# A fused attention and feed-forward backward pass: another opening on TensorE, and block-diagonal products without column tiles

## The chip, the core and the metric

The kernel runs on one core of a Trainium2 chip. The metric is the device time of one execution in microseconds (us); the median of the runs counts. The engines are TensorE (PE in the profile, its weight loads PEld), VectorE (DVE), ScalarE (ACT), GpSimd (POOL) and SyncE (SP, which issues most DMAs). TensorE writes its results to PSUM; a VectorE or ScalarE instruction copies them on to SBUF.

## The reference

The kernel computes a gated mix of a linear-attention block and a ReLU feed-forward block, together with all gradients. S is 2048, D is 640, there are 32 heads of 20, and the feed-forward width is 1728. All inputs are bf16.

```python
phi = lambda t: jnp.where(t > 0, t + 1, jnp.exp(t)) + 1e-6
q, k, v = split_heads(x @ wqkv)
pq, pk = phi(q), phi(k)
kv  = einsum("bhsd,bhse->bhde", pk, v);  z = einsum("bhsd->bhd", pk)
o   = einsum("bhqd,bhde->bhqe", pq, kv) / (einsum("bhqd,bhd->bhq", pq, z)[..., None] + 1e-6)
a   = merge_heads(o) @ wo
b   = relu(x @ w1) @ w2
g   = sigmoid((x * gate_w).sum(-1, keepdims=True))
out = g * a + (1 - g) * b
# outputs: out and its gradients for x, wqkv, wo, w1, w2, gate_w, given grad_out
```

## The kernel before

Rows of x are handled in 16 tiles of 128 (index `i`), columns of D in 5 chunks of 128 (index `k` or `m`). The work runs in stages, in this order: the key products of all 16 tiles (`k_part`) and two query tiles; the products of keys with x (`yp`); the forward blocks (`h_half`, `q_main`, `out_chunk`); the gradients of w2 (`w2p`); then the backward blocks, the gradients of w1, wq and wk, and that of x. Tiles in PSUM come from one pool, `PP`, with four buffers of two banks each: whoever wants a fifth waits until an earlier one has been copied out. Outside the opening the order of instructions on each engine is set by the framework's scheduler; each engine works through its own in order.

**The opening.** TensorE's order is written out by hand (L465 to L487, `manual_schedule`). It begins with products of a zeroed tile (`warm_up`, L445) that fill the time until data lands. `xt(i)` (L436) transposes the first five x tiles on TensorE: five transposes into a bf16 PSUM tile (`xtp`), then one copy to SBUF by `copy_out` (L347), on ScalarE for an even first argument and on VectorE otherwise. Between the warm-up and `xt(0)` stand one small transpose of the gate's weights (`gwtp`, L469) and a copy of five columns (L470) that makes the gate a 641st column of the key weights. `k_part(i, ks)` (L450) multiplies x tile `i` with the chunks `ks` of the key weights, 512 and 129 columns wide, accumulating in a PSUM tile `kp`. When a tile's last chunk is in, ScalarE takes two exponentials from it (L458 the gate, L395 in `phi_chain`), and VectorE finishes with L397 (bf16, SBUF to SBUF) and L398, which reads the PSUM tile a last time and so frees its buffer. The five chunks of the key weights are loaded one by one, 0 to 2 on ScalarE's queue and 3 and 4 on SyncE's. Tiles from 5 on are transposed by DMA (`xT_ld`); the first of these loads waits for `k_part(1, [2])`.

**GpSimd in the opening.** It builds the identity, then the masks of the heads: `MDw` (L493, L496 to L501) by 20 selects of 64x80, two for each 64-row half of a chunk, and `MDh` by 10 selects of 128x32 (L503, L505); nearly at the end it zeroes a matrix of 128x3200 (`KVT_s`, L507).

**Block-diagonal products.** Heads are 20 wide, so that a product of two 640x640 matrices is wanted only in blocks of 20 on the diagonal. `blockdiag` (L378) computes them by 64-row halves: for each chunk `m` and each `k`, two products with 64 stationary columns and 80 moving ones, which write partitions 0 to 63 and 64 to 127 of the same PSUM columns; VectorE multiplies the ten results with the mask (L390). It is called for `KVT_s` in the forward pass (L631) and for `dKVT_s` in `small_1` (L835).

**Window products.** `win_mms` (L366) multiplies with such a banded matrix: only the columns of each chunk's window (`WIN`: 0 to 140, 120 to 260, 240 to 400, 380 to 520, 500 to 640) are streamed. The 640 result columns are split at 320 over the two banks of a PSUM tile (`HD`), which cuts one window and gives six products of 140, 140, 80, 80, 140 and 140 columns. There are 20 such tiles: five in `mt_tile` (L634), five each in `small_0`, `small_2` and `small_3`. `halves` (L354) reads the two banks of 320 columns in one copy.

Of the kernel before, what the change touches and what calls it, by code (L numbers as in the profile page):

```python
# [8 lines left out]
ALU = mybir.AluOpType  # L9
AX = mybir.AxisListType  # L10
FP32 = mybir.dt.float32
BF16 = mybir.dt.bfloat16
PSUM = bass.MemoryType.PSUM

P = 128
H = 32
DH = 20
# [64 lines left out]
def kernel(  # L82
# [5 lines left out]
    nc = tc.nc  # L88
# [4 lines left out]
    S, D = x2.shape  # L93
    F = B_w1.shape[1]
    NT = S // P
    KD = D // P
# [6 lines left out]
    NG = NT // G  # L103
    assert NB * NBW == F and NB == 4 and D == H * DH and D % P == 0 and NT % 4 == 0 and FT < P
    WIN = _windows(D)
    BWID = max(-(-64 * (r + 1) // DH) * DH - 64 * r // DH * DH for r in range(2 * KD))
    DSPL = [(0, 512), (512, D)]
    DSP1 = [(0, 512), (512, D + 1)]
    DX = D + H
# [102 lines left out]
    xN = aview("xN", NT * DQX, i=NT)  # L212
    xN2 = aview("xN2", NT * D, i=NT)
    NPE = 5
# [7 lines left out]
    xTv = {i: (xT_view(i, i + 1), slice(0, P)) for i in range(NPE)}  # L222
# [8 lines left out]
    wk_s, wq_s, wv_s, wo_s = aview("wk", KD * DQX, k=KD), mat("wq"), mat("wv"), mat("wo")  # L231
# [5 lines left out]
    Y_s, YT_s, KVT_s, MT_s = mat("Y"), mat("YT"), mat("KVT"), mat("MT")  # L237
    M_s = aview("M", KD * D).rearrange("p (t c s) -> p t c s", t=KD, c=KD)
    dwoT_s, dwo_s = mat("dwoT"), mat("dwo")
    X_s, XT_s, woT_s, wvT_s, KV2_s = mat("X"), mat("XT"), mat("woT"), mat("wvT"), mat("KV2")  # L240
    dKV_s, dKVT_s, Q_s, N_s = mat("dKV"), mat("dKVT"), mat("Q"), mat("N")
# [19 lines left out]
    def gsl(i):  # L261
# [15 lines left out]
    cpool = ctx.enter_context(tc.tile_pool(name="const", bufs=1))  # L277
    tsb = ctx.enter_context(tc.tile_pool(name="ts", bufs=2))
    psp = ctx.enter_context(tc.tile_pool(name="ps", bufs=1, space=PSUM))
    ident = cpool.tile([P, P], BF16, name="ident")  # L280
    nc.gpsimd.memset(ident[:], 0.0)
    nc.gpsimd.affine_select(out=ident[:], in_=ident[:], compare_op=ALU.not_equal, fill=1.0, base=0,
                            pattern=[[-1, P]], channel_multiplier=1)
    gwb = cpool.tile([P, D], BF16, name="gwb")
    ones_sq = cpool.tile([P, P], BF16, name="ones_sq")
    zc_t = cpool.tile([P, KD], FP32, name="zc_t")
    MDw = cpool.tile([P, KD, BWID], BF16, name="MDw")
    MDh = cpool.tile([P, KD, H], BF16, name="MDh")
    zb = cpool.tile([P, D], BF16, name="zb")
    dzb = cpool.tile([P, D], BF16, name="dzb")  # L290
# [14 lines left out]
    def _nm(pfx):  # L305
        _cnt[0] += 1
        return f"{pfx}{_cnt[0]}"

    def pp(name="pp"):
        return psp.tile([P, 2, 512], FP32, tag="PP", bufs=4, name=_nm(name))  # L310
# [4 lines left out]
    def csl(i):  # L315
        return slice(i * P, (i + 1) * P)

    def flat(ps_tile):
        return ps_tile.rearrange("p b c -> p (b c)")
# [22 lines left out]
    def mm_cols(ps_tile, lhsT, rhs_fn, start, stop, spl=DSPL, **kw):  # L342
        for b, (a, e) in enumerate(spl):
            mm = nc.tensor.matmul(ps_tile[:, b, 0:e - a], lhsT=lhsT, rhs=rhs_fn(a, e), start=start, stop=stop, **kw)  # L344
        return mm

    def copy_out(n, dst, src):  # L347
        if n % 2 == 0:
            nc.scalar.copy(dst, src)  # L349
        else:  # L350
            nc.vector.tensor_copy(dst, src)

    HD = D // 2
    def halves(ap):  # L354
        return ap.rearrange("p (b c) -> p b c", b=2)

    SEGS = []
    for j, (lo, hi) in enumerate(WIN):
        if lo // HD == (hi - 1) // HD:
            SEGS.append((j, lo, hi))  # L360
        else:
            SEGS.append((j, lo, HD))
            SEGS.append((j, HD, hi))
    LASTSEG = {a // HD: n for n, (j, a, e) in enumerate(SEGS)}

    def win_mms(ps_tile, lhsT_fn, rhs_mat):  # L366

        seen = set()
        for n, (j, a, e) in enumerate(SEGS):
            bank = a // HD  # L370
            nc.tensor.matmul(ps_tile[:, bank, a - HD * bank:e - HD * bank], lhsT=lhsT_fn(j), rhs=rhs_mat[:, j, a:e],  # L371
                             start=bank not in seen, stop=LASTSEG[bank] == n, skip_group_check=True)
            seen.add(bank)

    HP = P // 2
    BW = [HP * r // DH * DH for r in range(2 * KD)]

    def blockdiag(dst, lhsT_mat, rhs_mat):  # L378

        ps = pp("bd")  # L380
        for m in range(KD):
            for k in range(KD):
                for h_ in range(2):
                    r = 2 * m + h_
                    nc.tensor.matmul(ps[h_ * HP:(h_ + 1) * HP, 0, m * BWID:(m + 1) * BWID],
                                     lhsT=lhsT_mat[:, k, r * HP:(r + 1) * HP], rhs=rhs_mat[:, k, BW[r]:BW[r] + BWID],
                                     start=(k == 0), stop=(k == KD - 1), skip_group_check=True)
        for r in range(2 * KD):
            m, hp = r // 2, slice(r % 2 * HP, r % 2 * HP + HP)
            nc.vector.tensor_tensor(dst[hp, m, BW[r]:BW[r] + BWID], ps[hp, 0, m * BWID:(m + 1) * BWID],  # L390
                                    MDw[hp, m, :], ALU.mult)

    def phi_chain(ps_flat, dst):
        eb = tmp("tb", 8)
# [39 lines left out]


    def xt(i):  # L436
        tp = psp.tile([P, KD, P], BF16, tag="PP", bufs=4, name=_nm("xtp"))
        for k in range(KD):
            nc.tensor.transpose(tp[:, k, :], xN[:, i, csl(k)], ident[:])
        copy_out(0 if i == 1 else 1, xTv[i][0], tp[:])  # L440

    def xT(i, k):
        return xTv[i][0][:, k, xTv[i][1]]

    def warm_up(n):  # L445
        for _ in range(n):
            nc.tensor.matmul(wp_[:, 0, :], lhsT=warm[:, 0:P], rhs=warm, start=True, stop=True)

    kps = {}

    def k_part(i, ks):
        if 0 in ks:
            kps[i] = pp("kp")
        kp = kps[i]
        for k in ks:
            mm = mm_cols(kp, xT(i, k), lambda a, e: wk_s[:, k, a:e], k == 0, k == KD - 1, spl=DSP1)
        if KD - 1 in ks:
            nc.scalar.activation(rg_t[:, i:i + 1], flat(kp)[:, D:D + 1], ACT.Exp, scale=-1.0)  # L458
            phi_chain(flat(kp)[:, 0:D], pkN[:, i, :])
            if i % 4 == 3:  # L460
                nc.sync.dma_start(pk_d[(i - 3) * P:(i + 1) * P, :].rearrange("(i p) d -> p i d", p=P),
                                  pkN[:, i - 3:i + 1, :])
        return mm

    wp_ = pp("warm")  # L465
    with tc.manual_schedule(engines={mybir.EngineType.PE}):
        warm_up(5)
        tp = psp.tile([P, KD, P], BF16, tag="PP", bufs=4, name="gwtp")
        nc.tensor.transpose(tp[:, 0, 0:KD], gst[:], ident[0:KD, 0:KD])  # L469
        nc.vector.tensor_copy(wk_s[:, :, D:D + 1], tp[:, 0, 0:KD].unsqueeze(2))  # L470
        xt(0)
        warm_up(2)
        k_part(0, [0])
        xt(1)
        k_part(0, [1])
        k_part(1, [0, 1])
        xt(2)
        k_part(0, [2])
        after(xT_ld[0], k_part(1, [2]), wait=True)
        k_part(2, [0, 1])  # L480
        k_part(0, [3, 4])
        xt(3)
        k_part(1, [3, 4])
        k_part(2, [2, 3, 4])
        xt(4)
        for i in range(3, NPE):
            k_part(i, range(KD))  # L487
    for i in range(NT):
        if i >= NPE:
            k_part(i, range(KD))  # L490
# [2 lines left out]
            nc.gpsimd.memset(MDw[:], 1.0)  # L493
            nc.gpsimd.memset(MDh[:], 1.0)

    for r in range(2 * KD):  # L496
        rel, md = HP * r - BW[r], MDw[r % 2 * HP:r % 2 * HP + HP, r // 2, :]
        nc.gpsimd.affine_select(out=md, in_=md, compare_op=ALU.is_ge, fill=0.0,
                                base=rel, pattern=[[-DH, BWID // DH], [0, DH]], channel_multiplier=1)
        nc.gpsimd.affine_select(out=md, in_=md, compare_op=ALU.is_ge, fill=0.0,  # L500
                                base=DH - 1 - rel, pattern=[[DH, BWID // DH], [0, DH]], channel_multiplier=-1)  # L501
    for j in range(KD):
        nc.gpsimd.affine_select(out=MDh[:, j, :], in_=MDh[:, j, :], compare_op=ALU.is_ge, fill=0.0,  # L503
                                base=P * j, pattern=[[-DH, H]], channel_multiplier=1)
        nc.gpsimd.affine_select(out=MDh[:, j, :], in_=MDh[:, j, :], compare_op=ALU.is_ge, fill=0.0,  # L505
                                base=DH - 1 - P * j, pattern=[[DH, H]], channel_multiplier=-1)
# [102 lines left out]
    for m in range(KD):  # L609
# [7 lines left out]
        if m == 2:  # L617
            tp = psp.tile([P, KD, P], BF16, tag="PP", bufs=4, name="w1ttp")
# [15 lines left out]
    def mt_tile(t):  # L634
        mp = pp("mtp")
        win_mms(mp, lambda j: wo_s[:, j, csl(t)], KVT_s)
        copy_out(t, halves(MT_s[:, t, :]), mp[:, :, 0:HD])

    mt_tile(0)
    mt_tile(1)  # L640
# [183 lines left out]
    def small_0():  # L824
        for t in range(KD):
            ps = pp("dwo")
            win_mms(ps, lambda m: X_s[:, m, csl(t)], KV2_s)
            copy_out(t, halves(dwoT_s[:, t, :]), ps[:, :, 0:HD])

    def small_1():  # L830
        nc.gpsimd.memset(dKVT_s, 0.0)  # L831
# [5 lines left out]
    def small_2():  # L837
        for t in range(KD):
            ps = pp("qqp")
            win_mms(ps, lambda j: wvT_s[:, j, csl(t)], dKVT_s)  # L840
            copy_out(t, halves(Q_s[:, t, :]), ps[:, :, 0:HD])

    def small_3():
        for t in range(KD):
            ps = pp("dwv")
            win_mms(ps, lambda j: YT_s[:, j, csl(t)], dKV_s)
            st = rnext("wst")
            nc.scalar.copy(halves(st), ps[:, :, 0:HD])
            nc.scalar.dma_start(out_2[csl(t), 2 * D:3 * D], st)


# [189 lines left out]
```

## Time and profile before

| what | value |
|---|---|
| three runs | 643.65, 643.67, 645.33 us; median 643.67 |
| profiled execution, device time | 643.67 us |
| its span, first to last instruction | 642.0 us |
| around the span | 1.67 us |
| TensorE busy | 634.3 us of the span (99%) |
| VectorE, ScalarE, GpSimd busy | 244.5, 151.2, 100.3 us |

Times in the profile are from the start of the span. A row of the timeline has the start, the length, the engine, the line, the operation, what it writes and reads, and in brackets how long the engine was idle before it and what released it. Successive instructions of one kind are merged into one row with a count (x5). A row's length for products reaches to the end of the last one's pipeline, so rows on TensorE overlap; the distance between two starts is the price of what lies between them. A row of the waits has the waiting engine, tile and line, then the releaser, then the total, the number and the longest, in us.

### The profile page before, as it was taken

The numbers are of one execution on the slowest core, as the hardware profiler recorded it, in microseconds if no ns is written. First come the engines' busy times: TensorE is split into PE (matmuls) and PEld (weight loads), VectorE is DVE, ScalarE is ACT, GpSimd is POOL, SyncE is SP. The second block draws the span as 40 slices with busy tenths as digits, with TensorE's granted clock in tenths as the row PEclk, the third lists the DMA queues.
The fourth block names the chain that finished last, engine by engine and source line by source line (L and its number), as shares of the span: only waits on it lengthen the run. The fifth ranks groups of instructions, "written<-read, shape, count | busy, mean of one in ns | idle before, by whom it ended". The sixth has DMA issues, their size and how long they took to land.

```text
span 642.0 us, 10598 instructions
## 1 busy us (share of the span) xinstructions
PE 634.3 (99%) x4492; PEld 352.9 (55%) x4492; DVE 244.5 (38%) x504; ACT 151.2 (24%) x223; POOL 100.3 (16%) x107
## 2 busy tenths in 40 slices
PE   7999999999999999999999999999999999999998
PEld 4555555555555555555555555555555555555554
DVE  4832754455445145555144332130016320104442
ACT  3522322122212123232143343531100011110000
POOL 6001633453235013222001000000000000000000
DMA  7998997543453953942979996892227549991111
GB/s 178 320 393 157 247 263 146 119 69 93 99 118 81 263 135 103 204 133 80 190 159 238 260 246 131 186 268 64 88 76 176 131 136 242 243 253 41 42 42 42
DMA packets 227075, 103.69 MB, mean 162 GB/s; under 512 B 183764, under 2 KB 226324, under 8 KB 227028
## 3 DMA queue, kind: packets, MB, share of 16 engines
q1 hardware_dynamic: 216602, 90.23, 60.2%
q10 hardware_dynamic: 10426, 12.78, 5.7%
q8 instruction: 35, 0.57, 0.4%
q14 instruction: 12, 0.10, 0.1%
HBM read 28.43 MB, written 28.84 MB: 89 GB/s over the span
## 4 chain that ended last, share of the span: by engine, by line
PE 93%; issue 4%; DVE 1%; ACT 1%; POOL 0%; POOLq 0%; DVEq 0%
PE w1p_4646 L882 1%; PE w1p_4777 L882 1%; PE w1p_5097 L882 1%; PE w1p_4874 L882 1%; PE w1p_4578 L882 1%; PE w1p_5290 L882 1%; PE w1p_5233 L882 1%; PE w1p_5165 L882 1%; PE w1p_5028 L882 1%; PE w1p_4709 L882 1%; PE op_2309 L344 1%; PE op_2272 L344 1%; PE op_2209 L344 1%; PE op_2172 L344 1%; PE op_2015 L344 1%
## 5 line engine op out<-in xcount | busy, mean ns | idle before, releaser
L344 PEld LDWEIGHTS <-arena 128*128 128x128 bf16 x2818 | 218.3, 98 | 171.4 <-DVE arena L398 1.9
L882 PEld LDWEIGHTS <-arena 128*128 128x128 bf16 x320 | 30.8, 98 | 26.9 <-issue 0.5
L795 PEld LDWEIGHTS <-arena 128*128 128x128 bf16 x320 | 30.5, 98 | 26.8 <-issue 1.3
L561 PEld LDWEIGHTS <-arena 128*128 128x128 bf16 x320 | 30.0, 98 | 26.7 <-issue 1.8
L866 DVE TENSOR_TENSOR tb_4852<-dkp_4841,dzb 128x640 bf16<-128x640 f32 x1 | 0.8, 825 | 41.5 <-PE dkp_4841 L344 41.5
L778 PEld LDWEIGHTS <-arena 128*128 128x128 bf16 x80 | 7.8, 98 | 9.6 <-issue 0.3
L970 PEld LDWEIGHTS <-arena 128*128 128x128 bf16 x80 | 7.8, 98 | 9.5
L983 DVE SCALAR_TENSOR_TENSOR f_5695<-gwb,dl_t,arena 128x640 f32<-128x640 bf16 x1 | 0.9, 886 | 26.7 <-ACT arena L964 26.7
L527 POOL TENSOR_TENSOR f_738<-tb_502,zb 128x640 f32<-128x640 bf16 x1 | 1.4, 1395 | 47.3 <-ACT zb L626 47.3
L371 PEld LDWEIGHTS <-arena 128*128 128x128 bf16 x120 | 7.0, 97 | 3.2 <-issue 2.4
L779 PEld LDWEIGHTS <-arena 128*128 128x128 bf16 x80 | 7.8, 98 | 0.0
L971 PEld LDWEIGHTS <-arena 128*128 128x128 bf16 x80 | 7.8, 98 | 0.0
L831 POOL MEMSET arena<- 128x3200 bf16 x1 | 2.8, 2764 | 30.4 <-ACT arena L349 30.4
L882 PE MATMUL w1p_4646<-arena 128*128 128x432 bf16 x32 | 6.0, 346 | 0.0
L882 PE MATMUL w1p_4777<-arena 128*128 128x432 bf16 x32 | 6.0, 346 | 0.0
L882 PE MATMUL w1p_4578<-arena 128*128 128x432 bf16 x32 | 6.0, 346 | 0.0
L882 PE MATMUL w1p_4874<-arena 128*128 128x432 bf16 x32 | 6.0, 346 | 0.0
L882 PE MATMUL w1p_5097<-arena 128*128 128x432 bf16 x32 | 6.0, 346 | 0.0
L882 PE MATMUL w1p_4709<-arena 128*128 128x432 bf16 x32 | 6.0, 346 | 0.0
L882 PE MATMUL w1p_5028<-arena 128*128 128x432 bf16 x32 | 6.0, 346 | 0.0
L882 PE MATMUL w1p_5165<-arena 128*128 128x432 bf16 x32 | 6.0, 346 | 0.0
L882 PE MATMUL w1p_5233<-arena 128*128 128x432 bf16 x32 | 6.0, 346 | 0.0
(1048 smaller groups left out, 1192.1 us busy)
## 6 DMA issues: line engine op xcount, KB each, us to landing
out_dram<-arena ACTq DMA_DIRECT2D x28, 160.0 KB, 2.8
arena<-in_A_x_dram SPq DMA_DIRECT2D x6, 640.0 KB, 6.3
pk_d<-arena SPq DMA_DIRECT2D x4, 640.0 KB, 9.5
arena<-in_grad_out_dram SPq DMA_DIRECT2D x4, 640.0 KB, 5.3
e_d<-arena SPq DMA_DIRECT2D x8, 320.0 KB, 2.5
out_dram<-arena ACTq DMA_DIRECT2D x8, 320.0 KB, 2.3
arena<-e_d SPq DMA_DIRECT2D x8, 320.0 KB, 3.8
dq_d<-arena SPq DMA_DIRECT2D x8, 320.0 KB, 3.6
```

The lines of the kernel that those rows point to most:

```text
L344: mm = nc.tensor.matmul(ps_tile[:, b, 0:e - a], lhsT=lhsT, rhs=rhs_fn(a, e), start=start, stop=stop, **kw)
L371: nc.tensor.matmul(ps_tile[:, bank, a - HD * bank:e - HD * bank], lhsT=lhsT_fn(j), rhs=rhs_mat[:, j, a:e], start=bank not in seen, stop=LA ...
L527: return nc.gpsimd.tensor_tensor(tzs[i][:], pqs[i][:], zb[:], ALU.mult)
L561: nc.tensor.matmul(hp[:, nb, 0:NBW], lhsT=xT(i, k), rhs=w1_s[:, k, blk * NBW:(blk + 1) * NBW], start=(k == 0), stop=(k == KD - 1))
L778: nc.tensor.matmul(xp[:, 0, :], lhsT=lhsT, rhs=doX(i)[:, 0:512], start=(i == 0), stop=(i == NT - 1))
L779: nc.tensor.matmul(xp[:, 1, 0:DX - 512], lhsT=lhsT, rhs=doX(i)[:, 512:DX], start=(i == 0), stop=(i == NT - 1))
L795: nc.tensor.matmul(gp[:, nb, 0:NBW], lhsT=doTg[i // G][:, k, gsl(i)], rhs=w2T_s[:, k, blk * NBW:(blk + 1) * NBW], start=(k == 0), stop=(k ...
L831: nc.gpsimd.memset(dKVT_s, 0.0)
L882: nc.tensor.matmul(wp[:, nb, 0:NBW], lhsT=xN2[:, i, csl(m)], rhs=hs(i)[:, blk * NBW:(blk + 1) * NBW], start=(i == 0), stop=(i == NT - 1))
L970: nc.tensor.matmul(wp[:, 0, :], lhsT=lhsT, rhs=dqN[:, i, 0:512], start=(i == 0), stop=(i == NT - 1))
L971: nc.tensor.matmul(wp[:, 1, 0:D + 1 - 512], lhsT=lhsT, rhs=dqN[:, i, 512:D + 1], start=(i == 0), stop=(i == NT - 1))
L983: nc.vector.scalar_tensor_tensor(base[:], gwb[:], dl_t[:, i:i + 1], dxB[:, i, :], ALU.mult, ALU.add)
```

## The change

It has three parts.

- The opening. `xt(0)` to `xt(2)` use plain matrix products with the identity as moving operand instead of transposes; their PSUM tile is f32 instead of bf16. `xt(0)` stands before the gate's transpose, and there are four warm-up products ahead instead of five. `xt(2)` stands ahead of the products of tile 1. The copies of tiles 2 and 4 are on ScalarE, those of 0, 1 and 3 on VectorE (before: tile 1 on ScalarE, the others on VectorE). Tiles 0 to 2 take key chunk 4 ahead of chunk 3. Two chunks of tile 3 stand ahead of the transposes of tile 4.
- `blockdiag` computes each chunk whole: 25 products with 128 stationary columns and 140 or 160 moving ones, and five multiplications with the mask. The mask `MDw` is 160 wide instead of 80, and GpSimd builds it by 10 selects of 128x160 instead of 20 of 64x80.
- `win_mms` splits its result at 512 instead of 320. That cuts two windows: seven products of 140, 140, 160, 132, 8, 12 and 128 columns. The copies read 640 columns in one piece, without `halves`.

```diff
-    HD = D // 2
-    def halves(ap):
-        return ap.rearrange("p (b c) -> p b c", b=2)
...
-        if lo // HD == (hi - 1) // HD:
+        if lo // 512 == (hi - 1) // 512:
...
-            SEGS.append((j, lo, HD))
-            SEGS.append((j, HD, hi))
+            SEGS.append((j, lo, 512))
+            SEGS.append((j, 512, hi))
...
+    BD_POS = [(0, j * WMAX) if j < 3 else (1, (j - 3) * WMAX) for j in range(KD)]
     def blockdiag(dst, lhsT_mat, rhs_mat):
         ps = pp("bd")
-        for m in range(KD):
+        for m, (lo, hi) in enumerate(WIN):
+            bk, off = BD_POS[m]
             for k in range(KD):
-                for h_ in range(2):
-                    r = 2 * m + h_
-                    nc.tensor.matmul(ps[h_ * HP:(h_ + 1) * HP, 0, m * BWID:(m + 1) * BWID],
-                                     lhsT=lhsT_mat[:, k, r * HP:(r + 1) * HP], rhs=rhs_mat[:, k, BW[r]:BW[r] + BWID],
-                                     start=(k == 0), stop=(k == KD - 1), skip_group_check=True)
-        for r in range(2 * KD):
-            m, hp = r // 2, slice(r % 2 * HP, r % 2 * HP + HP)
-            nc.vector.tensor_tensor(dst[hp, m, BW[r]:BW[r] + BWID], ps[hp, 0, m * BWID:(m + 1) * BWID],
-                                    MDw[hp, m, :], ALU.mult)
+                nc.tensor.matmul(ps[:, bk, off:off + hi - lo], lhsT=lhsT_mat[:, k, csl(m)], rhs=rhs_mat[:, k, lo:hi],
+                                 start=(k == 0), stop=(k == KD - 1), skip_group_check=True)
+        for m, (lo, hi) in enumerate(WIN):
+            bk, off = BD_POS[m]
+            nc.vector.tensor_tensor(dst[:, m, lo:hi], ps[:, bk, off:off + hi - lo], MDw[:, m, 0:hi - lo], ALU.mult)
...
     def xt(i):
-        tp = psp.tile([P, KD, P], BF16, tag="PP", bufs=4, name=_nm("xtp"))
+        if i < 3:
+            tp = flat(pp("xtp"))[:, 0:D].rearrange("p (k s) -> p k s", k=KD)
+        else:
+            tp = psp.tile([P, KD, P], BF16, tag="PP", bufs=4, name=_nm("xtp"))
         for k in range(KD):
-            nc.tensor.transpose(tp[:, k, :], xN[:, i, csl(k)], ident[:])
-        copy_out(0 if i == 1 else 1, xTv[i][0], tp[:])
+            if i < 3:
+                nc.tensor.matmul(tp[:, k, :], lhsT=xN[:, i, csl(k)], rhs=ident[:], start=True, stop=True,
+                                 skip_group_check=True)
+            else:
+                nc.tensor.transpose(tp[:, k, :], xN[:, i, csl(k)], ident[:])
+        copy_out(0 if i in (2, 4) else 1, xTv[i][0], tp)
...
-        warm_up(5)
+        warm_up(4)
+        xt(0)
         tp = psp.tile([P, KD, P], BF16, tag="PP", bufs=4, name="gwtp")
         nc.tensor.transpose(tp[:, 0, 0:KD], gst[:], ident[0:KD, 0:KD])
         nc.vector.tensor_copy(wk_s[:, :, D:D + 1], tp[:, 0, 0:KD].unsqueeze(2))
-        xt(0)
         warm_up(2)
         k_part(0, [0])
         xt(1)
         k_part(0, [1])
+        xt(2)
         k_part(1, [0, 1])
-        xt(2)
         k_part(0, [2])
         after(xT_ld[0], k_part(1, [2]), wait=True)
-        k_part(2, [0, 1])
-        k_part(0, [3, 4])
+        k_part(2, [0, 1, 2])
+        k_part(0, [4, 3])
         xt(3)
-        k_part(1, [3, 4])
-        k_part(2, [2, 3, 4])
+        k_part(1, [4, 3])
+        k_part(2, [4, 3])
+        k_part(3, [0, 1])
         xt(4)
-        for i in range(3, NPE):
-            k_part(i, range(KD))
+        k_part(3, [2, 3, 4])
+        k_part(4, range(KD))
...
-    for r in range(2 * KD):
-        rel, md = HP * r - BW[r], MDw[r % 2 * HP:r % 2 * HP + HP, r // 2, :]
-        nc.gpsimd.affine_select(out=md, in_=md, compare_op=ALU.is_ge, fill=0.0,
-                                base=rel, pattern=[[-DH, BWID // DH], [0, DH]], channel_multiplier=1)
-        nc.gpsimd.affine_select(out=md, in_=md, compare_op=ALU.is_ge, fill=0.0,
-                                base=DH - 1 - rel, pattern=[[DH, BWID // DH], [0, DH]], channel_multiplier=-1)
     for j in range(KD):
+        rel = P * j - WIN[j][0]
+        nc.gpsimd.affine_select(out=MDw[:, j, :], in_=MDw[:, j, :], compare_op=ALU.is_ge, fill=0.0,
+                                base=rel, pattern=[[-DH, WMAX // DH], [0, DH]], channel_multiplier=1)
+        nc.gpsimd.affine_select(out=MDw[:, j, :], in_=MDw[:, j, :], compare_op=ALU.is_ge, fill=0.0,
+                                base=DH - 1 - rel, pattern=[[DH, WMAX // DH], [0, DH]], channel_multiplier=-1)
...
-        copy_out(t, halves(MT_s[:, t, :]), mp[:, :, 0:HD])
+        copy_out(t, MT_s[:, t, :], flat(mp)[:, 0:D])
```

The order on the engines moves with it. On VectorE the gate's small copy now stands behind the copy of tile 0, and the ten maskings become five in the same place. On ScalarE the copy of tile 2 stands where that of tile 1 stood, and the copy of tile 4 behind the exponential of tile 2. On GpSimd the selects of both masks are interleaved in another order: nine of 128x160 and nine of 128x32 stand ahead of the 128x3200 memset, and one of each behind it; before, 20 of 64x80 and nine of 128x32 stood ahead and one of 128x32 behind. SyncE's order is unchanged.

## The prediction

> **What bounds the kernel now.** I read the page's engine shares and chain first, then TensorE's waits, then the timeline of the places that the change touches.
>
> ```profile
> span 642.0 us, 10598 instructions
> PE 634.3 (99%) x4492; PEld 352.9 (55%) x4492; DVE 244.5 (38%) x504; ACT 151.2 (24%) x223; POOL 100.3 (16%) x107
> PE 93%; issue 4%; DVE 1%; ACT 1%; POOL 0%; POOLq 0%; DVEq 0%
> ```
>
> TensorE carries 93% of the chain that ended last. So a microsecond that TensorE gains or loses anywhere should reach the end, and work on other engines counts only where TensorE waits for it. Those places are few (engine, line, releaser: us in total, times, longest):
>
> ```profile
> PE kp_228 L344 <- DVE arena L398: 1.8, 1, 1.8
> PE warm_129 L447 <- DVE arena L402: 1.3, 1, 1.3
> PE mtp_850 L371 <- DVE arena L390: 0.6, 2, 0.3
> PE kp_161 L344 <- ACT arena L349: 0.5, 1, 0.5
> PE qp_874 L344 <- ACT arena L349: 0.2, 1, 0.2
> ```
>
> Two lie in the opening (kp_161, kp_228), two around the first block-diagonal product (mtp_850, qp_874). The longest, in the timeline (start, us):
>
> ```profile
> 9.62 2.76 POOL L507 MEMSET arena<- 128x3200 bf16 x1
> 9.90 0.70 ACT L395 ACTIVATE tb_187<-kp_149 128x640 bf16<-128x640 f32 x1
> 10.63 1.93 DVE L397 TENSOR_SCALAR tb_189<-tb_187 128x640 bf16<-128x640 bf16 x1
> 12.59 0.82 DVE L398 SCALAR_TENSOR_TENSOR arena<-kp_149,tb_189 128x640 bf16<-128x640 f32 x1
> 336.90 2.76 POOL L831 MEMSET arena<- 128x3200 bf16 x1 [30.45 <-ACT arena L349]
> 337.41 2.52 DVE L801 TENSOR_SCALAR tb_3614<-arena 128x864 bf16<-128x864 bf16 x1
> ```
>
> L397 takes 0.33 us for its other tiles; here it takes 1.93 and ends 0.18 after GpSimd's memset ends (12.38). L801 (usually 0.38) is stretched in the same way by the same memset at 337. A long GpSimd memset thus holds up such an SBUF-to-SBUF VectorE operation; a copy out of PSUM at 10.11 kept its 0.49 beside it. So key tile 0 leaves PSUM at 13.41, and the fourth key tile, which needs its buffer, starts at 13.47, 1.76 late.
>
> **Opening, up to the fourth key tile.** The first x load is issued at 0.81 and lands 2.2 later, at 3.0. Four warm-up products instead of five (0.43 each from 1.26) end at 2.97, so the transposes of tile 0 start near 3.05 instead of 3.62. Five take 0.5 at this speed, as before. The copy out is now from f32: 0.82 (L351 from mtp_858) instead of 0.49. It ends near 4.6, the gate's little copy (0.18) near 4.8; the first key chunk, issued at 1.40, lands 3.3 later, at 4.7. The first key product starts at 4.77, not 4.98. Tile 1's copy is now 0.82 on VectorE instead of 0.69 on ScalarE, so tile 1's products, which waited 0.5 for it, start at 6.92 instead of 6.94. Tile 2's transposes now fill that wait, and the 0.2 before kp_177 (8.53) goes too. At 0.272 per chunk (1.36 per tile of five), tile 0 is complete at 9.38 instead of 9.63, and all of tiles 0 to 2 plus two chunks of tile 3 at 11.29. Chunks 4 and 3, issued at 2.20 to 3.1 and 3.7 us in landing, are there by 6.9, so their order costs and saves nothing. No DMA is added or moved; names and lines from here on that the profile doesn't have are those of the changed program.
>
> Then the transposes of tile 4 wait for tile 0's buffer, with the last three chunks of tile 3 and all of tile 4 queued behind them. ScalarE's exponential ends at 10.35 (0.97 after the products, as now). The rest depends on the memset, now L506. Ahead of it stand 9 mask selects of 128x160 and 9 of 128x32, instead of 20 of 64x80 and 9 of 128x32, and a memset of 800 columns instead of 400 (+0.33, by 2.76 for 3200 and 0.45 for 400). No row shows 128x160. Bounds: 0.29 (the 128x128 identity) and 0.60 (twice 64x80's spacing of 0.30); I take 0.39, since 32 columns take 0.206 and 80 take 0.264. The selects then begin at 2.22 and the memset at 2.22+9x0.39+9x0.19=7.4, ending at 10.2, and with some gaps between dependent selects at 10.4: just when VectorE wants L389. Then 0.33, 0.82 and 0.1 of handing over: tile 4's transposes start at 11.7. Five transposes (0.28), three chunks (0.82) and a wait of 0.1 for ScalarE's copy (0.69) put tile 4 at 12.93 and tile 5 at 14.29; before, tile 5 began at 16.21. Gain 1.92; with selects of 0.60 the memset ends at 12.1 and the gain is 0.4; with quicker ones 1.98, as the exponential then binds. What is late next: the transposing loads wait for tile 1's third chunk (8.2, before 8.52, so they land 0.3 earlier), tile 5 needs theirs at 14.3 (landed 13.3 before), and the query weights, landed at 27.7, are needed at 29.4.
>
> **Clock.** In the timeline the array's speed doubles inside xtp_152, a transpose:
>
> ```profile
> 5.51 0.64 PE L439 MATMUL xtp_152<-ident,arena 128*128 128x128 bf16 x5
> 6.00 0.44 PE L344 MATMUL kp_149<-arena 128*128 128x512 bf16 x2
> ```
>
> kp_149's first pair took 0.53, this second one 0.27. I leave the moment of full speed at 5.9. Were it at 4.8, the 1.1 us from the first key product on would shrink by half, 0.5 or so, of which the memset takes back what it outlasts the exponential by. The Trainium skill ("TensorE: Matmul & The Clock Gate", part 4) says that transposes don't count as busy for the clock, so that by it plain products could bring full speed earlier; the row, where full speed comes amid transposes, doesn't show that they delay it.
>
> **First block-diagonal product.**
>
> ```profile
> 62.06 1.09 PE L385 MATMUL bd_775<-arena 128*64 128x80 bf16 x50
> 63.08 2.00 PE L561 MATMUL hp_836<-arena 128*128 128x432 bf16 x10
> 63.67 2.53 DVE L390 TENSOR_TENSOR arena<-bd_775,MDw 64x80 bf16<-64x80 f32 x10
> 67.25 1.52 PE L344 MATMUL qp_874<-arena 128*128 128x512 bf16 x10 [0.21 <-ACT arena L349]
> ```
>
> Fifty products take 1.02, about 0.02 each: the two halves run beside each other. The new 25 stream 3600 columns at 0.425 ns (0.272 for 641): 1.55. TensorE loses 0.53. VectorE's masking falls from ten pieces of 0.238 to five: 640 columns from f32 take 0.82 and 80 take 0.238, so 140 take 0.30 and five 1.6 in all instead of 2.5. It ends at 65.4, before hp_795 ends (63.61+1.84=65.45), so both waits of mtp_850 (0.56) vanish, three window tiles end by 66.55, ScalarE's copy frees a buffer at 66.7, and qp_836 starts at 66.78 instead of 67.25: gain 0.47. Two more window tiles give back 0.1.
>
> **Window tiles.** Six products of 720 columns take 0.32 (mtp_891 at 68.61, mtp_899 at 68.93). The split at 512 makes seven of the same 720 columns, of 8 and 12 columns among them. If those run by their columns, nothing is added; if like 80 columns (0.035), 0.06; I take 0.05. The same page, part 1, gives a floor of 25 ns from start to start for however narrow a product; by it the two narrow ones add an estimated 0.04 a tile, which speaks against the change. In each of the later three uses, tiles four and five wait for a copy (335.73, 336.32), which hides the first ones' part: 0.05 each, 0.15 in all, 0.9 if nothing hides it.
>
> **Second block-diagonal product (355.5).** TensorE waits for nothing there, so its 0.53 is lost in full; VectorE's 0.9 helps nobody.
>
> **Sum.** -1.92 -0.47 +0.10 +0.53 +0.15 = -1.61. The profiled run took 643.67 (span 642.0 and 1.67 around it), which is also the median: 642.06, put at 642.1. About 0.3%, or 1.9 us, is what a measurement here can tell from no change.
>
> **Rivals.**
> - *More than 0.3% faster.* The memset is gone by 9.8, full speed comes early (up to 0.5), and the narrow products cost nothing: -1.98-0.5-0.47+0.53=-2.4, 641.3. For it: the fits of the selects allow 9.3. Against it: the exponential then binds, and an early clock must coincide. 0.25.
> - *Slow selects.* With 0.60 the opening gains 0.4 only, the sum is -0.1, 643.6. Eight rows of 20 in place of four speak for it, the small step from 32 to 80 columns against it. 0.15.
> - *Slower.* Full speed comes later than 5.9. Before, the memset hid up to 1.8 us of that (tile 0's exponential ended at 10.6, the memset at 12.38). Now nothing does: each us later costs 0.5. From 3.2 us later (9.1) the sum is above zero, and if the opening stays at half speed to its end (7 us later) it is +1.9: 645.6. For it: one of the three runs took 645.33, 1.7 more than the others. Against it: TensorE is as busy as before from 1.26 on. 0.12, of which 0.07 for more than 0.3%.
> - *The order of chunks does nothing*: part of the forecast, as all have landed.
>
> **How the numbers follow.** The forecast itself (-1.0 to -1.9) has 0.48; it, the slow selects and half of the slower case lie within 0.3%: 0.68. Range: 641.4 takes in part of the first rival, 644.0 slow selects with a late clock or window tiles at 0.06 unhidden.
>
> **What would show it.** L506 ends before 10.6 and L389's first run is near 0.33; the longest wait of TensorE is 0.3 to 0.5, at xtp_225 on L390; tile 5 starts near 14.3; mtp waits for no L383; 25 products take 1.55. I am wrong if L506 ends after 11.5, if key products still take twice their time after 7 us, or if a wait for a transposing load appears at tile 5 or 8.

## The result, and the profile after

| | median, us | lowest to highest | runs |
|---|---|---|---|
| before | 643.68 | 643.65 to 645.33 | 6 |
| changed | 641.77 | 641.42 to 643.25 | 6 |

The ratio is 0.9965, with a 95% interval of 0.9949 to 0.9980: 0.35% faster, at the edge of what the prediction called no change. Two of the six runs of before took 645.33, the other four agree to 0.04. The profiled execution is the slowest of the six, 643.25 us with a span of 641.5; the other five have spans of 639.7 to 640.2. That difference has to be explained too, and two more profiles of the same kernel were taken for it.

The page of the changed kernel:

```profile
span 641.5 us, 10518 instructions
PE 636.5 (99%) x4461; PEld 355.5 (55%) x4461; DVE 241.0 (38%) x493; ACT 152.0 (24%) x224; POOL 98.6 (15%) x97
PE 98%; DMA 1%; ACT 1%; DVE 0%; issue 0%; ACTq 0%
```

TensorE still carries the chain, now 98% of it. Its waits, in the same columns as before:

```profile
PE warm_129 L446 <- DVE arena L394: 1.3, 1, 1.3
PE kp_148 L344 <- DMA arena<-in_A_wqkv_dram: 0.3, 1, 0.3
PE xtp_225 L438 <- DVE arena L390: 0.3, 1, 0.3
```

The wait of 1.8 on tile 0 has become 0.3, and both waits around the first block-diagonal product are gone. In the timeline of the opening:

```profile
6.62 2.77 POOL L506 MEMSET arena<- 128x3200 bf16 x1
7.46 1.25 PE L344 MATMUL kp_167<-arena 128*128 128x512 bf16 x4
9.04 0.50 PE L344 MATMUL kp_167<-arena 128*128 128x512 bf16 x2
9.38 0.98 PE L344 MATMUL kp_176<-arena 128*128 128x512 bf16 x6
11.01 0.70 ACT L387 ACTIVATE tb_188<-kp_148 128x640 bf16<-128x640 f32 x1
11.74 0.33 DVE L389 TENSOR_SCALAR tb_190<-tb_188 128x640 bf16<-128x640 bf16 x1
12.10 0.82 DVE L390 SCALAR_TENSOR_TENSOR arena<-kp_148,tb_190 128x640 bf16<-128x640 f32 x1
13.07 0.44 PE L438 MATMUL xtp_225<-ident,arena 128*128 128x128 bf16 x5 [0.25 <-DVE arena L390]
15.67 1.53 PE L344 MATMUL kp_266<-arena 128*128 128x512 bf16 x10
336.42 2.48 DVE L800 TENSOR_SCALAR tb_3583<-arena 128x864 bf16<-128x864 bf16 x1
```

The memset ends at 9.39, long before VectorE wants L389, which takes its usual 0.33. But in this execution the array reached full speed only between 9.04 and 9.38: the pair of kp_167 still took 0.34, the next ones 0.272. So tile 5 (kp_266) starts at 15.67 instead of 16.21, a gain of only 0.54. L800, stretched by the later memset as before, shows that the memset still blocks where the two meet.

The first block-diagonal product, then the second:

```profile
59.60 1.99 PE L560 MATMUL hp_743<-arena 128*128 128x432 bf16 x10
61.43 1.73 PE L379 MATMUL bd_764<-arena 128*128 128x140 bf16 x25
62.99 1.99 PE L560 MATMUL hp_795<-arena 128*128 128x432 bf16 x10
63.19 1.17 DVE L383 TENSOR_TENSOR arena<-bd_764,MDw 128x140 bf16<-128x140 f32 x5
66.11 1.52 PE L344 MATMUL qp_836<-arena 128*128 128x512 bf16 x10
...
354.37 1.73 PE L379 MATMUL bd_3740<-arena 128*128 128x140 bf16 x25
355.93 1.99 PE L794 MATMUL gp_3771<-arena 128*128 128x432 bf16 x10
```

The 25 products take 1.56 us (61.43 to 62.99) where 50 in pairs took 1.02, and nothing waits afterwards. From hp_743 to qp_836 there are 6.51 us; before, hp_754 at 60.14 to qp_874 at 67.25 made 7.11.

### The profile page after: what moved, and what is told of

Read it like the earlier page. It is cut to its first block, busy times and chain, and to the rows that moved or that the text cites. A ratio compares the mean times of both kernels' runs of the same rounds, so it can differ in the third digit from the quotient of the medians.

```text
span 641.5 us, 10518 instructions
## 1 busy us (share of the span) xinstructions
PE 636.5 (99%) x4461; PEld 355.5 (55%) x4461; DVE 241.0 (38%) x493; ACT 152.0 (24%) x224; POOL 98.6 (15%) x97
## 4 chain that ended last, share of the span: by engine, by line
PE 98%; DMA 1%; ACT 1%; DVE 0%; issue 0%; ACTq 0%
PE w1p_4726 L881 1%; PE w1p_4595 L881 1%; PE w1p_5239 L881 1%; PE w1p_5182 L881 1%; PE w1p_4977 L881 1%; PE w1p_4527 L881 1%; PE w1p_5114 L881 1%; PE w1p_5046 L881 1%; PE w1p_4823 L881 1%; PE w1p_4658 L881 1%; PE op_2273 L344 1%; PE op_2236 L344 1%; PE op_2173 L344 1%; PE op_2136 L344 1%; PE op_1942 L344 1%; PE op_1590 L344 1%
```

## Experiments

**1. The new opening alone.** The kernel before with `xt`, `k_part` and the hand-written order of the changed one; masks, block-diagonal and window products as before.

> The kernel before with the new opening alone; masks, block-diagonal products and window products as before. My theory: most of the gain came from GpSimd's 128x3200 memset ending earlier (9.4 instead of 12.4 us), because fewer mask selects stand ahead of it, not from TensorE's new order. Here the memset ends at 12.4 again, so VectorE's L397 for tile 0 ends at 12.6, tile 4's transposes start at 13.5 and tile 5 near 16.05 (16.21 before): 0.15 us faster than before, 643.5. Rival: the order of TensorE and the plain products bring it; then tile 5 starts near 14.3 and the time is 641.8, less the part of the block-diagonal products: 641.7.

Measured: 643.61 us (643.65 before; ratio 1.0007, 0.9998 to 1.0016). Three of its eleven runs took 645.1 to 645.3, the other eight agree to 0.05. The timeline has the old wait:

```profile
9.62 2.76 POOL L515 MEMSET arena<- 128x3200 bf16 x1
10.39 2.18 DVE L397 TENSOR_SCALAR tb<-tb 128x640 bf16<-128x640 bf16 x1
13.57 0.44 PE L446 MATMUL xtp<-ident,arena 128*128 128x128 bf16 x5 [2.10 <-DVE arena L398]
```

TensorE gets to tile 4 earlier and waits 2.1 us there for the same memset. The part of the change that names the opening moved nothing by itself.

**2. The new products alone.** The changed kernel with the opening of before, so the new masks, block-diagonal and window products.

> The changed kernel with the opening of before (transposes, old order, old copies), so the new masks, block-diagonal products and window products alone. My theory: the memset ends near 9.4, L397 for tile 0 takes 0.33 from 10.63 on, tile 0's buffer is free at 11.85 and tile 3 starts at 11.9 instead of 13.47: 1.6 gained in the opening. The rest as seen between the two profiles: first block-diagonal product -0.60, two window tiles +0.08, second product +0.45, later window tiles +0.15, together +0.08. Sum -1.5: 642.15. Rival (TensorE's order brings the gain): 643.7, as before.

Measured: 642.21 us (0.9975, 0.9965 to 0.9984), 1.44 faster; 642.15 had been expected.

```profile
6.63 2.76 POOL L498 MEMSET arena<- 128x3200 bf16 x1
10.68 0.33 DVE L389 TENSOR_SCALAR tb<-tb 128x640 bf16<-128x640 bf16 x1
11.93 2.30 PE L344 MATMUL kp<-arena 128*128 128x512 bf16 x15 [0.16 <-DVE arena L390]
```

Tile 3 starts at 11.93 where it started at 13.47. Ten wide selects in place of 20 narrow ones, ahead of the memset, are enough for that. Against the whole change (641.77) 0.44 is missing, less than the spread of either kernel's runs (641.60 to 643.08 here): what the new opening adds once the memset is out of the way can't be told.

**3. The memset first.** The kernel before with one line moved:

```diff
             nc.gpsimd.memset(MDh[:], 1.0)
+            nc.gpsimd.memset(KVT_s, 0.0)
...
-    nc.gpsimd.memset(KVT_s, 0.0)
```

> The kernel before with one line moved: the 128x3200 memset on GpSimd stands ahead of the mask selects, so it runs from 1.9 to 4.7 us and the selects end near 12.4. My theory: only the memset holds up VectorE's L397; tile 3 starts at 11.9 instead of 13.47 and the time falls by 1.6 to 642.1. Rival: any GpSimd instruction holds L397 up, so it crawls between selects of 0.26 to 0.3 us: tile 3 at 12.2 or later, 642.4 or more; if each operand access waited, L397 would take over 1 us and the gain would be under 0.8.

Measured: 641.74 us (0.9972, 0.9960 to 0.9983): as fast as the whole change, by a line that the change doesn't touch. L397 runs among the selects:

```profile
10.04 0.27 POOL L499 TENSOR_SCALAR_AFFINE_SELECT MDw<-MDw 64x80 bf16<-64x80 bf16 x1
10.11 0.38 DVE L397 TENSOR_SCALAR tb<-tb 128x640 bf16<-128x640 bf16 x1
10.37 0.71 POOL L504 TENSOR_SCALAR_AFFINE_SELECT MDh<-MDh 128x32 bf16<-128x32 bf16 x4
11.40 2.30 PE L344 MATMUL kp<-arena 128*128 128x512 bf16 x15 [0.21 <-DVE arena L398]
```

It takes 0.38 instead of 0.33, so selects cost it 0.05 at most. That this goes by the length of the GpSimd instruction, and not by its being a memset, is borne out by another place in the kernel before, where a long TENSOR_TENSOR on GpSimd meets a VectorE operation of the same kind, which usually takes 0.34:

```profile
71.12 1.39 POOL L527 TENSOR_TENSOR f_931<-tb_885,zb 128x640 f32<-128x640 bf16 x1 [3.39 <-DVE tb_885 L398]
71.69 1.01 DVE L545 TENSOR_SCALAR tb_928<-tb_519 128x640 bf16<-128x640 bf16 x1
```

It ends at 72.70, 0.19 after the GpSimd instruction, as L397 ended 0.18 after the memset. The gain of experiment 3 was 0.3 above what was expected; in this profile the trace's record of the granted clock has full speed from 4.42 already.

**4. Transposes into bf16 again.** The changed kernel, but tiles 0 to 2 are transposed as before:

```diff
-        if i < 3:
-            tp = flat(pp("xtp"))[:, 0:D].rearrange("p (k s) -> p k s", k=KD)
-        else:
-            tp = psp.tile([P, KD, P], BF16, tag="PP", bufs=4, name=_nm("xtp"))
+        tp = psp.tile([P, KD, P], BF16, tag="PP", bufs=4, name=_nm("xtp"))
         for k in range(KD):
-            if i < 3: ...
-            else:
-                nc.tensor.transpose(tp[:, k, :], xN[:, i, csl(k)], ident[:])
+            nc.tensor.transpose(tp[:, k, :], xN[:, i, csl(k)], ident[:])
```

> The changed kernel with tiles 0 to 2 transposed by TensorE's transpose into bf16 again, all else as changed. My theory: the copy out of bf16 takes 0.49 instead of 0.82 on VectorE, tile 1's products start 0.33 earlier, tile 0 is complete 0.33 earlier, and VectorE is free of the memset since 9.4: 0.3 us faster than the changed kernel, 641.4 by its median of 641.8. Rival (transposes don't count as busy for the clock): full speed comes one window of 3.4 us later in all or most runs, 1.7 us lost: 643.1.

Measured: 641.71 us (641.10 to 642.10), 0.06 from the changed kernel's median. The rival is out: nothing near 1.7 us is lost, and full speed came here between 6.4 and 6.8. The 0.3 expected from shorter copies can't be told from the spread of either kernel. So plain products instead of transposes are worth nothing that these runs can tell. The Trainium skill ("TensorE: Matmul & The Clock Gate", part 4) has transposes not count as busy for the clock; no run here shows that.

**5 and 6. The changed kernel twice more**, one execution each, for their profiles.

> The changed kernel once more, for a second profile. My theory: the profile of the changed kernel took 643.25 because the array came to full speed at 9.2 us only; the moment is free, so here it should lie elsewhere between 4.4 and 9.2, and with full speed near 6 tile 5 starts near 14.3 and the run takes 641.5. For every us that full speed comes earlier than 9.2, tile 5 starts 0.5 us earlier, down to about 14.2, where VectorE's work on tile 0 binds. Rival: the late opening is this kernel's own (its gap before the first key product): full speed at 9.2 and 643.2 again.

> The changed kernel a third time, with the same expectations: another moment of full speed, and tile 5 and the time moving with it at half a us for each us. Rival: full speed at 9.2 and 643.2 again.

Measured: 642.10 and 642.07 us, spans of 640.4 both. The moment of full speed is read from the rows of the key products; first the fifth, then the sixth run:

```profile
6.07 0.57 PE L344 MATMUL kp<-arena 128*128 128x512 bf16 x2
6.48 0.44 PE L435 MATMUL xtp<-ident,arena 128*128 128x128 bf16 x5
7.20 2.57 PE L344 MATMUL kp<-arena 128*128 128x512 bf16 x17 [0.28 <-DVE arena L351]
```

```profile
6.39 0.74 PE L435 MATMUL xtp<-ident,arena 128*128 128x128 bf16 x5
6.98 2.76 PE L344 MATMUL kp<-arena 128*128 128x512 bf16 x17
```

The five products that transpose a tile take 0.44 at full speed and 0.74 at half. So full speed came between 6.1 and 6.5 in one, and near 7.4 in the other (the clock's record begins at 7.39); in the first profile at 9.17. The moment is free.

The two runs, a us apart in it, took the same time all the same. In the fifth the first chunk of key weights landed at 5.0 and the first key product started at 5.05, against 4.81 in the sixth. At full speed TensorE then waited 0.28 for tile 1's f32 copy on VectorE, so that tile 1's products started at 7.20. In the sixth they started at 6.98 and ran at half speed for another 0.41, which costs 0.2. In the first profile the chunk landed at 5.28, the first key product started at 5.32, tile 1's products (kp_167) at 7.46, and half speed lasted 1.71 from there. Against the sixth run that makes 0.48 by the later start and 0.65 by the longer half speed, 1.13 together; the first query product came 1.12 later (30.66 against 29.54), and the execution took 1.18 more. So half a us for each us counts from the start of tile 1's products on; before it, the wait for the copy takes the gain back.

**7. The memset twice.** The kernel before with the memset line doubled, to lengthen the wait.

> The kernel before with the 128x3200 memset done twice: the second runs from 12.6 to 15.4 us and holds up VectorE's L397 for tile 1, behind which the copy of tile 4's transposes stands, so tile 4 starts at 16.25 instead of 14.85. By the waits alone: 1.4 us slower, 645.05. My theory of the runs of before that took 645.3: the wait of 1.8 us lets the array fall back to half speed for one window of 3.4 us, which costs 1.7 more; with 3.2 us of waiting between 11.6 and 16.2 that should come in most runs: 646.7, and the profile shows products of twice the length for 3.4 us after the wait. Rival: the array keeps its speed, 645.05 in nearly all runs.

Measured: median 644.83 (1.0032, 1.0019 to 1.0045), eight runs of twelve between 644.82 and 644.87, three at 647.6 and one at 648.27. By the waits alone 645.05 had been expected: right. "Most runs" for the second effect was wrong, a third had it. The profiled run was one of the eight; TensorE waited 1.9 and 0.9 us in it and the array kept its speed. The run at 648.27 lost 3.4; what made it the slowest is open.

**8. Mixed.** Experiment 4 with the first block-diagonal product whole, the second by pairs (masked with slices of the wide mask), and window products split at 320:

```diff
-        blockdiag(dKVT_s, woT_s, XT_s)
+        blockdiag_pairs(dKVT_s, woT_s, XT_s)
...
+                                    MDw[hp, m, BW[r] - WIN[m][0]:BW[r] - WIN[m][0] + BWID], ALU.mult)
```

> The best of both by the stages: the new opening with transposes into bf16, the first block-diagonal product whole, the second by pairs of 64-row halves (masked with slices of the wide mask), the window products split at 320 as before. Against the run with the transposes (641.7): second product 0.45 less, 20 window tiles at 0.04 each of which 0.25 on the path: 641.0. Against the kernel before: 2.65 us faster. Rival: the window split and the second product are hidden by waits: 641.6.

Measured: 640.44 us (0.9952, 0.9940 to 0.9964), 3.3 faster than before: the fastest kernel of this case. From the start of the first block-diagonal product to the end of the span it takes 639.10-59.77 = 579.33, experiment 4 takes 639.98-59.95 = 580.03: 0.70 less, as the two terms said (0.45 and 0.25). Of the lead of the profiled execution (0.88 in the span) the other 0.18 lies ahead of that product, in the opening. The medians lie 1.27 apart; the 0.4 that this leaves is no more than the openings spread, and no profile shows where it lies.

**9. Pairs in both places.** The same with `blockdiag_pairs` for the first product too.

> The mixed kernel with both block-diagonal products by pairs of 64-row halves. My theory: the first product's 25 whole matrix products cost TensorE 0.53 us more than 50 in pairs, but the pairs' ten maskings make it wait; the whole version was 0.6 ahead between the two profiles, so 0.6 is lost here: 641.0 (640.4 for the mixed kernel). Rival: the waits would vanish anyway once the opening has changed; then the pairs save 0.53: 639.9.

Measured: 641.71 us (0.9969, 0.9958 to 0.9981), 1.27 behind the mixed kernel instead of 0.6. From the first product on the difference is 640.02-60.13 = 579.89 against 579.33, 0.56, and the waits are back:

```profile
PE mtp L372 <- DVE arena L405: 0.6, 2, 0.3
PE qp L345 <- ACT arena L350: 0.2, 1, 0.2
```

The sign and the stage's 0.56 speak for the theory; the other 0.7 of the medians is of the size by which the openings spread, and isn't traced (in this profile alone tile 0's second product waited 1.0 for its chunk of key weights).

**10 to 12. The memset twice, three more profiles.** The tenth's expectation says five runs of twelve; there were four.

> The kernel with two memsets once more, for a profile of a run near 647.6 us (five of twelve runs took that or more, the others 644.8). If the array falls back to half speed, the profile shows products of twice the usual length for one or two windows of 3.4 us after the waits. If it shows full speed throughout, the lost 2.7 us are somewhere else and the stages will tell where. A run of 644.8 tells nothing new.

> The kernel with two memsets a third time, with the expectations of the last run: products of twice the usual length after the waits if it is a run near 647.6, nothing new if it is one near 644.8.

> The kernel with two memsets a fourth time, with the expectations of the last two runs: products of twice the usual length after the waits if it is a run near 647.6, nothing new if it is one near 644.8.

Measured: 647.52, 644.85 and 644.80 us. The first is one of those that lose 2.7 us. Its key products at the two waits, then stretches of it (start and end, length, the busy time of the five engines, then PEclk, the granted clock, and two columns on DMA):

```profile
13.48 1.65 PE L344 MATMUL kp<-arena 128*128 128x512 bf16 x10 [2.23 <-DVE arena L398]
15.97 8.31 PE L344 MATMUL kp<-arena 128*128 128x512 bf16 x39 [0.83 <-DVE arena L351]
```

```profile
13.50:16.00 2.50, 1.67 (x11) 0.75 (x12) 2.50 (x3) 0.77 (x2) 1.83 (x1) 0.75 0.96 218
16.00:17.00 1.00, 1.00 (x4) 0.44 (x5) 0.96 (x3) 0.00 (x0) 0.00 (x0) 0.50 0.83 102
18.00:20.00 2.00, 2.00 (x9) 1.01 (x8) 1.15 (x2) 0.77 (x2) 0.00 (x0) 0.50 0.99 190
21.00:23.00 2.00, 2.00 (x13) 1.03 (x12) 0.56 (x2) 0.77 (x2) 0.00 (x0) 0.85 1.06 376
```

The clock's record has full speed from 4.52, half from 14.76 to 21.59, and full again to the end. So the array fell back 1.3 us after the end of the wait of 2.23, and before the wait of 0.83 began at 15.14; it stayed at half speed for 6.83 us, and the query products start 2.7 us later than in the seventh run (35.07 against 32.37). In the other two profiles, and in the seventh run's, it doesn't fall. There the first wait is shorter (1.47, 1.68 and 1.95): its end, near 13.5, is set by the memset, and TensorE comes to it later because full speed came later (6.77, 6.24 and 5.63). In experiment 1's profile a wait of 2.10 passed without a fall. How long a wait must be is not shown by one fall.

## Why the prediction was right, and where it was not

The forecast was 642.1 with a range of 641.4 to 644.0; 641.77 lies in it. Its steps:

| step | predicted, us | measured, us |
|---|---|---|
| memset on GpSimd ends at | 10.4 | 9.39 |
| L389 for tile 0 takes | 0.33 | 0.33 |
| wait of tile 4's transposes | 0.3 to 0.5 | 0.25 |
| opening (to the first query product) | -1.92 | -0.54; -1.63 and -1.66 in experiments 5 and 6 |
| first product, hp to qp | -0.47 | -0.60 |
| two window tiles | +0.10 | +0.08 |
| second product | +0.53 | +0.45 |
| later window tiles | +0.15 | +0.15 |
| sum; measured: time against before | -1.61 | -0.42 in the profile; -1.57 and -1.60 in experiments 5 and 6 |

The central step, that the wait on tile 0 was GpSimd's memset and that fewer selects ahead of it would take the wait away, is shown from three sides: the opening without the new masks gains nothing (1), the masks without the opening gain 1.4 (2), the memset moved gains all (3). That the new opening adds something of its own once the memset is gone is not shown (2). The price of the 128x160 selects, for which no row stood, was the widest term. They take 0.37 each, and since the next one begins before the last row's end, 18 selects took 4.39 instead of the 5.2 summed. That error cost nothing, because ScalarE's exponential binds once the memset is gone by 10.4, as the prediction said.

The maskings were too dear in the sum: five take 1.17, not 1.6 (0.29 each, but started 0.21 to 0.23 apart). That gained nothing, as they end before hp_795 does in the forecast too. Both block-diagonal products came out better than forecast (0.13 and 0.08), and some 0.09 of each has a reason for which the prediction had no term: the first pair of column tiles starts 0.09 later than a whole product does. In the second use it starts 0.150 after the product before it, where the whole one starts 0.056 after it; in the first use, behind a product of 432 columns, it is 0.275 in experiment 9 against 0.182 in experiment 8. The 25 products themselves were priced right (1.56; 3600 columns at 0.425 ns are 1.53, not the 1.55 written).

The narrow window products of 8 and 12 columns start 0.029 and 0.025 before the next one, and a tile takes 0.356 instead of 0.317: 0.04 more, where I took 0.05. The floor of 25 ns from start to start that the Trainium skill states ("TensorE: Matmul & The Clock Gate", part 1) agrees with these rows. The waits for copies hid the rest as predicted: the three later groups lost 0.04, 0.04 and 0.07.

The step that failed is the clock. I held full speed at 5.9, the moment of one profile, and gave a late one 0.12. Over the profiles here it came between 4.4 and 9.2 us. In the very execution profiled the third rival's mechanism was at work, 3.3 us late, and the sign of being wrong that I had named, key products at twice their time after 7 us, was there. The opening ended 1.38 later than forecast (tile 5 at 15.67 instead of 14.29): tile 1's products started at 7.46 instead of 6.92, by the late landing of the first key chunk, and half speed lasted 1.71 from there, which costs 0.86. In experiments 5 and 6 tile 5 started at 14.59 and 14.56, 0.3 late.

The rival's price was wrong as well. It had the sum at zero for a clock 3.2 us late, at half a us for each us from 5.9 on. But by the prediction's own working tile 1's products wait until 6.92 for their copy, so only what lies behind that counts: 1.1 for a clock at 9.17, not 1.6. So the profiled execution stayed 0.42 ahead of before.

What the rival said about before was right: its runs agree to 0.1 us (643.64 to 643.70, 20 of 22 beside experiments 1 to 4) because the memset, which starts by GpSimd's time and not by TensorE's, hid the moment of full speed. Experiments 1 and 7, which keep the wait for the memset, have eight runs each within 0.05; experiments 2 and 3, which don't, spread over 1.5 and 0.7. Of the changed kernel's eight runs (six, and experiments 5 and 6) no such cluster is left: 641.4 to 643.3.

Part of the close sum is luck. In experiments 5 and 6 the opening gained 0.3 less than forecast, and the block-diagonal products and window tiles 0.2 more. All three profiles of the changed kernel lie above its median; where the runs at 641.4 to 641.95 gained more than the forecast is not shown.

## What to carry to other kernels

A long GpSimd instruction, here a memset, is not free just because GpSimd has nothing else to do: find the first SBUF-to-SBUF VectorE instruction that meets it and is waited for, and put the memset well ahead of it. When a change moves several engines, look on each of them for what moved; here ten mask selects on GpSimd brought what the rewritten order on TensorE did not. A stage that is bound by one engine's fixed time hides the jitter of the others, so when that bound falls, take several profiles before believing one. A shorter form on TensorE (pairs of column tiles) can still lose where the copies behind it are more and smaller, and win where nobody waits for them.

## What the runs showed of the hardware that I had not expected

- The array can lose its full speed after a wait of 2.2 us: in the one profile that caught it, half speed began 1.3 us after that wait and lasted 6.83 us. In five of 15 executions of the kernel with two memsets 2.7 us or more were lost. The Trainium skill ("TensorE: Matmul & The Clock Gate", part 1) tells of a free-running window of 3.4 us: 6.83 is two of them, and the 10.24 us of full speed before it are three. But by its table an idle window brings the fall, and here no wait was as long as a window.
- The rare runs of before at 645.3 us, 1.7 above the rest (two of 6, two of 22, one of 17, none of 11; three of 11 in experiment 1), fit the same cause with half the length. Where the mean granted clock is on record for them it is 0.997, against 0.999 to 1.000 for the others. In the profiled fall 6.83 us at half speed make 0.995; by that, 0.997 is an estimated 3.2 to 4.5 us at half speed, and 3.4 of them would cost the 1.7. No profile caught one, so where it lies in the run is open.
- The moment of full speed after the start was between 4.4 and 9.2 us, for kernels whose TensorE starts at 1.26 in all of them.
- The landing of the first key chunk let the first key product start anywhere from 4.8 to 5.3 in three executions of one kernel.
- Going over to pairs of column tiles and back has a price. The first pair starts 0.09 later than a whole product would, and the next whole product starts 0.134 after the start of the last pair's (63.08 in the profile of before), against 0.061 after a whole product of 140 columns.
